# Relu² attention and a gated feed-forward layer on one core: the seventh batch's regrouping pieces stand 11 passes later in the fifth batch's part

## The chip, the cores and the metric

The kernel runs on one core of a Trainium2 chip. The metric is the time of one execution on the device in microseconds. The kernel before took 402.35 us, the median of three runs (401.11 to 404.22).

## The reference

There are 8 batches, 12 heads, 448 tokens and a head size of 64, so the feed-forward layer has 3584 tokens, a width of 768 and a hidden size of 1536. Inputs and output are float32.

```python
scores = scale * np.matmul(q, k.transpose(0, 1, 3, 2))
attn = np.maximum(scores, 0.0) ** 2 / S
attn_out = np.matmul(attn, v)
x = attn_out.transpose(0, 2, 1, 3).reshape(B * S, H * D)
gate = np.maximum(x @ w_gate, 0.0)
val = x @ w_val
out = gate * val @ w_out
```

## The kernel before

**The five engines.** TensorE (PE) multiplies matrices into PSUM banks; VectorE (DVE) and ScalarE (ACT) compute on and evict them; GpSimd (POOL) and SyncE (SP) mostly issue transfers. Each engine works through its own instructions in the order in which the kernel pins them (`pin`, line 68), and waits where an instruction's inputs are not there.

**Parts.** The loop over b, from 1 to 6, at lines 762 to 808, makes one part for each b. In part b PE computes the gate and value products of batch b-1 in 12 units (`gv_unit`, line 302), one for each 128 hidden columns. A unit is 12 passes, and a pass is four matmuls of 64 by 64 weights on 448 tokens (`mm4`, line 79). At its end ACT takes the relu of the gate (line 320) and DVE multiplies it with the value half into `hT` (line 321). Units take the PSUM bank pairs 6 and 4 in turn. Counted from zero, unit 9 and unit 11 therefore share a pair.

**Events.** Between the passes stand the attention's steps, each at a place (unit, pass). A score tile is one pass of matmuls from `kqT`, the transposed k and q, a relu by ACT (line 232) and a square by DVE (line 233). Seven of them make one group of four heads; a value event then runs seven passes of v on these squares, evicts them by ACT and DVE (lines 266 and 267) and exchanges halves with two DVE copies (line 261). `paced` spreads score and value events evenly over the part; `spread` sorts all events by place, keeping the order of those at the same place, and puts each ahead of that pass. In the part b = 4, called the fifth batch's part here, the fifth batch's scores and the first seven score tiles of the sixth are computed, and a last value event stands at (11, 5).

**Loads, regrouping and transposes.** From the third batch on, k and q come into `kn` and `qn` by POOL's transfers. Four regrouping pieces for a batch turn them: each is one DVE copy of half of k or q into `kr` or `qr` (`regroup`, line 180, 128 by 1536 elements), followed on SP's queue by two transposing transfers into `kqT` (`transpose_grouped`, line 188). `turned` places a batch's four pieces: two for k at a given place and five passes later, and two for q at another place and five passes later. `hold` (line 691) makes POOL read an element at the end of both halves of `kqT`, so that POOL issues the next batch's loads only when the transposes have landed. In the part b = 4, `hold(5)` and the load of the seventh batch's k and q (`load_qk(6)`) are placed at (5, 4), and the seventh batch's pieces behind them. The next part (b = 5) has `hold(6)` and the next load at (2, 1).

**The output products.** Behind part b = 4 stands `out_pair(2, ...)`, the output products of two batches in seven products for each 128 tokens instead of eight. Its products take PSUM banks 6, 7, 0, 1 and 2, 3, 4, 5. DVE makes the sums of `hT` for it (line 349): first S1 = A21 + A22, then S3 = A11 - A21 and S2 = S1 - A11. PE's first eight products need no sum; the next four use S2. ACT and DVE evict the results (lines 395 and 399), and POOL and SP store them (line 409).

Of the kernel before, what the change touches and what calls it, by code (L numbers as in the profile page):

```python
# [16 lines left out]
def kernel(  # L17
# [122 lines left out]
    def load_qk(b, h0=0, h1=H):  # L140
        load_nat(kn_b[natural(b)], k, b, h0, h1)
        load_nat(qn_b[natural(b)], q, b, h0, h1)

    def load_v(b):
        for c, p in HALVES:
            if b == 0:
                src = v[b].rearrange("(g c h) s d -> c h g s d", c=2, h=2)[c]
                dst = v_b[b % NB][p].rearrange("p (g h) i d -> p h g i d", h=2)
                parts = [(dst[:, h2], src[h2]) for h2 in range(2)]
            else:  # L150
                parts = [(v_b[b % NB][p], v[b, c * HP:c * HP + HP])]
            for dst, src in parts:
                dma_in(dst[:, :, 0:4, :], src[:, 0:256, :].rearrange("g (j i) d -> j g i d", i=4))
                dma_in(dst[:, :, 4:7, :], src[:, 256:448, :].rearrange("g (j i) d -> j g i d", i=3))
# [12 lines left out]
    def load_wo():  # L167
        for c in range(2):
            rows = moe_w_out[c * (d_ff // 2):(c + 1) * (d_ff // 2), :]
            dma_in(wo_sb[c], rows.rearrange("(kf p) m -> p kf m", p=128))  # L170
# [5 lines left out]
    def regroup(b, t, h):  # L176

        nat, grp = ((kn_b[natural(b)], kr), (qn_b[natural(b)], qr))[t]
        i = slice(2 * h, 2 * h + 2)
        pin(nc.vector.tensor_copy(grp.rearrange("p i (h d) -> p i h d", d=D)[:, i],  # L180
                                  nat.rearrange("p h i d -> p i h d")[:, i]))

    def transpose_grouped(b, t, h):

        grp = (kr, qr)[t]
        for i in (2 * h, 2 * h + 1):
            r = 128 if i < 3 else 64
            pin(nc.sync.dma_start_transpose(out=T_b[b % NB][:, t, :, i * 128:i * 128 + r], in_=grp[0:r, i, :]))
# [103 lines left out]
    def flat(t, n, c):  # L292

        names = " ".join("abcd"[:len(t.shape) - 1])
        return t.rearrange(f"p {names} -> p ({names})")[:, 0:n * c].rearrange("p (n c) -> p n c", c=c)

    def new_x(b):
        x = [xpool.tile([128, HP, S], BF16, name=f"x{n}") for n in range(2)]
        x_of[b] = [quads(t) for t in x]
        return x  # L300
# [40 lines left out]
    def weight_sums(n):  # L341

        o, a, b, op = ((T1, B12, B11, ALU.subtract), (B12, B22, B12, ALU.subtract),
                       (T2, B22, T1, ALU.subtract), (T4, B21, T2, ALU.subtract))[n]
        pin(nc.vector.tensor_tensor(o, a, b, op))
# [239 lines left out]
    def gv_units(b):  # L585
        b0 = b - b % 2
        if b == b0:
            hT_of[b0] = hpool.tile([128, KF, 2 * S], BF16, name="hT")
        return [gv_unit(b, mf, BEGUN, rotation((BEGUN_IN[mf],))) if b == 0 and mf < len(BEGUN_IN) else
                gv_unit(b, mf, BEGUN if mf == 0 else STRAIGHT, acc) for mf in range(KF)]  # L590
# [85 lines left out]
    def values_event(b, qd):  # L676
        return lambda: (values_by_parity if b >= B - 2 else values)(b, qd, sc_later())

    def transposes_event(b, qd):
        return lambda: transpose_quad(b, qd)  # L680
# [7 lines left out]
    def hold(b):  # L688

        for t in range(2):  # L690
            pin(nc.gpsimd.tensor_copy(flag[:, t:t + 1], T_b[b % NB][:, t, HP - 1, S - 1:S]))  # L691
# [26 lines left out]
    def step(units, u, n, k):  # L718
        at = len(units[-1]) * u + n + k
        return at // len(units[-1]), at % len(units[-1])  # L720

    def turned(b, units, *at):

        def piece(t, h):
            regroup(b, t, h)
            transpose_grouped(b, t, h)
        return [(*step(units, u, n, 5 * h), lambda t=t, h=h: piece(t, h)) for t, (u, n) in enumerate(at) for h in range(2)]

    def stream(b0, b1):

        e = []
        for b in range(b0, b1):
            for n in range(NT):
                if n % NC == 2 and (b, n) != (b0, 2):
                    vb, qd = (b, n // NC - 1) if n > NC else (b - 1, NQ - 1)
                    e.append((b, n, values_event(vb, qd), NC))
                e.append((b, n, scores_event(b, n), 1))
        return e

    def paced(units, first, behind, events):  # L740

        at = [(u, n) for u in range(len(units)) for n in range(len(units[u]))][first:behind]
        gaps = [{(1, 1): 1, (1, NC): 0.35, (NC, 1): 0.75}[a[3], b[3]] for a, b in zip(events, events[1:])]
        gap = len(at) / (sum(gaps) + 1)
        places, due = [], gap / 2
        for (*_, e, _), g in zip(events, gaps + [0]):
            u, n = at[int(due)]
            places.append((u, n, e))
            due += g * gap
        return places  # L750
# [5 lines left out]
    units = gv_units(0)  # L756
# [5 lines left out]
    for b in range(1, B - 1):  # L762
        if b < B - 3:
            new_x(b)
        units = units[2:] if b == 1 else gv_units(b - 1)
        last = len(units) - 1
        if b < B - 4:
            first, behind = {1: (24, 105), 2: (40, 132)}.get(b, (0, 132))
            events = paced(units, first, behind, stream(b, b + 1))
            events.append((last, 8 if b == 1 else 5, values_event(b, NQ - 1)))  # L770
        else:
            todo = [e for e in attention if e[:2] <= ENDS[b]]
            del attention[:len(todo)]
            if b == B - 4:
                begun = flat(kn_b[1], 4, S)
                x_of[b + 1] = [[begun[:, 2 * e:2 * e + 2, :]] for e in range(2)]
                del attention[[e[3] for e in attention].index(NC)]
            events = paced(units, 0, 144 if b == B - 3 else 132, todo)
            if b != B - 3:
                events.append((last, 5, values_event(*((b + 1, 0) if b == B - 4 else (B - 1, NQ - 1)))))  # L780
        if b == 1:
            events += [(1, 2 + 4 * qd, transposes_event(1, qd)) for qd in range(NQ)]
            events += turned(2, units, (last - 3, 7), (last - 2, 7))
            events += [(last, 2, lambda: (hold(2), load_v(2), load_wo(), load_qk(3)))]
        elif b == 2:
            events += [(1, 1, lambda: load_v(3))]
            events += [(last - 5 + 2 * n, 6, lambda n=n: weight_sums(2 * n)) for n in range(2)]
            events += [(last - 1 + t, 3 + 5 * h, lambda t=t, h=h: regroup(3, t, h)) for t in range(2) for h in range(2)]
            events += [(last, 10, lambda: [transpose_grouped(3, t, h) for t in range(2) for h in range(2)])]
        elif b == 3:  # L790
            events += [(2, 1, lambda: (hold_unit(2, 1), hold(3), load_qk(4), load_v(4)))]
            events += turned(4, units, (6, 1), (7, 1)) + [(8, 4, lambda: (hold(4), load_qk(5)))]
        elif b == 4:
            events += [(0, 4, lambda: load_v(5))]
            events += turned(5, units, (2, 1), (3, 1)) + [(5, 4, lambda: (hold(5), load_qk(6)))]
            events += turned(6, units, (last - 2, 6), (last - 1, 6))
        elif b == 5:
            events += [(2, 1, lambda: (hold_unit(4, 1), load_v(6), hold(6), load_qk(7)))]
            events += turned(7, units, (last - 4, 6), (last - 3, 6))
            later = [xpool.tile([128, HP, S], BF16, name=f"x{n}") for n in range(2)]  # L800
            x_of[b] = [x_of[b][e] + quads(later[e])[1:] for e in range(2)]
            x_of[B - 2] = [quads(t)[:1] for t in later]
        elif b == 6:
            events += [(3, 1, lambda: (hold(7), load_v(7)))]
            new = [xpool.tile([128, HP, S], BF16, name=f"x{n}") for n in range(2)]
            x_of[b] = [x_of[b][e] + quads(new[e])[1:] for e in range(2)]
            x_of[B - 1] = [quads(flat(t, HP, S)) for t in (kr, qr)]
        spread(units, events)
        if b == 2:
            out_pair(0, flat(kn_b[1], KH, S), [lambda: weight_sums(1), lambda: weight_sums(3)])  # L810
        elif b == 4:
            out_pair(2, flat(v_b[0], KH, S))
# [48 lines left out]
```

## Time and profile before

| | before |
|---|---|
| median of 3 runs | 402.35 us (401.11 to 404.22) |
| profiled execution, its own time | 403.33 us |
| its span, first to last instruction | 401.6 us |
| PE / DVE / ACT / POOL busy | 97% / 75% / 61% / 24% of the span |
| granted TensorE clock | 1.00 |
| DVE's regrouping copies, 24 of 128 by 1536 elements | 0.55 us each |

The profile shows one execution. Times in it are microseconds from the start of the span. PE, DVE, ACT, POOL and SP are the engines, and a q behind the name (SPq) means its queue of issued work. L180 is line 180 of the kernel. In a row of a timeline stand the start, the length, the engine and line, the operation, what it writes and reads, and how many instructions the row merges; in brackets stands the idle time of the engine just before it and what ended it. "issue" there means that the profile shows nothing that was waited for; a wait for a transfer's landing can hide behind it. A matmul's row ends when its last result is written; the next pass can start before that, so rows of PE overlap.

### The profile page before, as it was taken

To read this page: it belongs to the slowest core of one execution; us is meant where nothing else is said; L and a number is where in the kernel's file an instruction comes from. 1 tells how busy PE (TensorE), PEld (TensorE's weight loads), DVE (VectorE), ACT (ScalarE), POOL (GpSimd) and SP (SyncE) were. 2 spreads that over 40 slices of the span, in tenths; PEclk is the share of its full clock that TensorE was granted. 3 is DMA by queue.
4 is the path that set the end of the run, shared out by engine and by line. 5 is a ranking of instruction groups with operands and counts; after the bars stand their busy time and mean duration, and the time that the engine had idled before them with its cause. 6 is when DMAs were issued, how large, how long until landed. Compare 5 with 4: busy or idle time off the path is not lost.

```text
span 401.6 us, 16574 instructions
## 1 busy us (share of the span) xinstructions
PE 389.9 (97%) x7376; PEld 290.5 (72%) x7376; DVE 302.9 (75%) x530; ACT 243.6 (61%) x358; POOL 96.3 (24%) x168
## 2 busy tenths in 40 slices
PE   7899999999999999999899999999999999999995
PEld 3466779978776666679677666988887766777664
DVE  4985896699944696887781478988889969997922
ACT  3962994787334776988533588899883234344231
POOL 7933300810213600503031360020003230000223
PEclk9999999999999999999999999999999999999999
DMA  9999998999836894997963588770002350000036
GB/s 151 168 196 197 196 191 97 155 205 179 135 83 179 108 163 82 149 154 86 171 110 80 160 108 103 122 89 4 4 2 52 77 153 3 2 3 3 20 83 177
DMA packets 90872, 44.17 MB, mean 110 GB/s; under 512 B 55424, under 2 KB 89792, under 8 KB 90800
## 3 DMA queue, kind: packets, MB, share of 16 engines
q0 software_dynamic: 51264, 28.83, 50.5%
q1 hardware_dynamic: 39104, 13.99, 19.8%
q8 instruction: 57, 0.93, 1.0%
q10 hardware_dynamic: 432, 0.30, 0.3%
q14 instruction: 15, 0.12, 0.1%
HBM read 47.19 MB, written 11.01 MB: 145 GB/s over the span
## 4 chain that ended last, share of the span: by engine, by line
PE 86%; DMA 5%; DVE 5%; issue 1%; ACT 1%; POOL 1%; ACTq 0%; DVEq 0%; POOLq 0%
PE ps L72 85%; DMA qn<-in_q_dram 5%; DVE attn L233 2%; ACT r_sb L232 1%; PE ps L208 1%; DVE kqT L209 1%; POOL kn L116 1%; POOL qn L116 0%; DVE x L267 0%; DVE hT L321 0%; DVE r_sb L630 0%; DVE x L653 0%; PE ps L217 0%; DVE x L261 0%; ACT g_sb L320 0%
## 5 line engine op out<-in xcount | busy, mean ns | idle before, releaser
L72 PE MATMUL ps<-x,gv 64*64 64x448 bf16 x3408 | 198.4, 349 | 1.2 <-DVE hT L321 0.9
L72 PEld LDWEIGHTS <-gv 64*64 64x64 bf16 x4032 | 150.5, 107 | 44.5 <-issue 2.9
L232 ACT ACTIVATE r_sb<-ps 128x896 bf16<-128x896 f32 x167 | 149.0, 933 | 17.7 <-PE ps L72 15.0
L233 DVE TENSOR_TENSOR attn<-r_sb 128x896 bf16<-128x896 bf16 x167 | 101.9, 622 | 29.2 <-ACT r_sb L232 22.0
L409 POOL DMA_DIRECT2D out_dram<-attn x63 | 33.1, 530 | 170.0 <-DVE attn L399 134.6
L72 PE MATMUL ps<-kqT 64*64 64x448 bf16 x672 | 68.6, 351 | 3.4 <-ACT r_sb L232 2.6
L72 PEld LDWEIGHTS <-hT 128*64 128x64 bf16 x1056 | 55.9, 110 | 20.9 <-issue 1.4
L395 ACT ACTIVATE attn<-ps 128x384 f32<-128x384 f32 (+1 forms) x64 | 28.8, 450 | 64.3 <-PE ps L72 63.3
L72 PE MATMUL ps<-wo,hT 128*64 128x384 bf16 (+1 forms) x720 | 54.3, 306 | 0.0
L321 DVE TENSOR_TENSOR hT<-ps,g_sb 128x448 bf16<-128x448 f32 x72 | 44.5, 619 | 8.3 <-ACT g_sb L320 7.5
L320 ACT ACTIVATE g_sb<-ps 128x448 bf16<-128x448 f32 x72 | 39.2, 546 | 17.3 <-PE ps L72 17.1
L399 DVE TENSOR_TENSOR attn<-ps,attn 128x384 f32<-128x384 f32 (+1 forms) x48 | 22.8, 503 | 33.0 <-ACT attn L395 18.4
L72 PEld LDWEIGHTS <-vn 64*64 64x64 bf16 (+1 forms) x888 | 35.8, 107 | 12.3 <-issue 2.3
L72 PEld LDWEIGHTS <-kqT 64*64 64x64 bf16 x672 | 28.3, 106 | 14.1 <-issue 6.0
L72 PE MATMUL ps<-attn,vn 64*64 64x448 bf16 x672 | 37.8, 350 | 0.7 <-DVE attn L233 0.7
L528 ACT ACTIVATE kqT<-ps 128x896 f32<-128x896 f32 x18 | 16.5, 918 | 25.0 <-PE ps L72 25.0
L116 POOL DMA_DIRECT2D vn<-in_v_dram x36 | 23.7, 678 | 17.8 <-PE ps L72 5.8
L72 PE MATMUL ps<-o_ring,hT 128*64 128x384 bf16 (+1 forms) x336 | 26.0, 306 | 0.0
L532 DVE TENSOR_TENSOR kqT<-ps,kqT 128x896 f32<-128x896 f32 x18 | 19.5, 1086 | 5.9 <-PE ps L72 4.2
L691 POOL COPY flag<-kqT 128x1 bf16<-128x1 bf16 x12 | 2.2, 197 | 89.7 <-DMA kqT<-kr 48.3
L116 POOL DMA_DIRECT2D qn<-in_q_dram x20 | 14.8, 762 | 1.3 <-POOLq L845 0.8
L261 DVE COPY x<-x 64x896 bf16<-64x896 bf16 x34 | 13.5, 397 | 1.8
(101 smaller groups left out, 288.5 us busy)
## 6 DMA issues: line engine op xcount, KB each, us to landing
out_dram<-attn POOLq DMA_DIRECT2D x48, 96.0 KB, 2.3
out_dram<-attn SPq DMA_DIRECT2D x48, 96.0 KB, 2.6
kn<-in_k_dram POOLq DMA_DIRECT2D x7, 384.0 KB, 6.8
qn<-in_q_dram POOLq DMA_DIRECT2D x7, 384.0 KB, 9.2
vn<-in_v_dram POOLq DMA_DIRECT2D x14, 192.0 KB, 8.8
gv<-in_moe_w_gate_dram POOLq DMA_DIRECT2D x6, 384.0 KB, 11.6
gv<-in_moe_w_val_dram POOLq DMA_DIRECT2D x6, 384.0 KB, 11.8
wo<-in_moe_w_out_dram POOLq DMA_DIRECT2D x2, 1152.0 KB, 13.7
```

The source lines that it names most:

```text
L72: pin(nc.tensor.matmul(o, lhsT=l, rhs=r, start=start, stop=stop, skip_group_check=True))
L116: pin(nc.gpsimd.dma_start(out=o, in_=i))
L232: pin(nc.scalar.activation(r, src, AF.Relu))
L233: pin(nc.vector.tensor_tensor(dst, r, r, ALU.mult))
L261: pin(nc.vector.tensor_copy(x1[p], x0[other]))
L320: pin(nc.scalar.activation(g_sb, o[0], AF.Relu, scale=float(out_scale)))
L321: pin(nc.vector.tensor_tensor(hT[:, mf, col:col + S], o[1], g_sb, ALU.mult))
L395: pin(nc.scalar.activation(out_of(t, r, c), bank(P, t), AF.Copy))
L399: pin(nc.vector.tensor_tensor(o, bank(Q, t), o, ALU.add))
L409: pin(engines[c].dma_start(out=rows[:, c0:c1, :], in_=src))
L528: pin(nc.scalar.activation(held(n, j), both(PQ[n][0]), AF.Copy))
L532: pin(nc.vector.tensor_tensor(k, both(PQ[n][1]), k, ALU.add))
```

## The change

One line differs, in the part b = 4. `last` is 11, the number of the last unit.

```diff
             events += turned(5, units, (2, 1), (3, 1)) + [(5, 4, lambda: (hold(5), load_qk(6)))]
-            events += turned(6, units, (last - 2, 6), (last - 1, 6))
+            events += turned(6, units, (last - 1, 5), (last, 5))
```

The pieces for k move from the places (9, 6) and (9, 11) to (10, 5) and (10, 10); those for q move from (10, 6) and (10, 11) to (11, 5) and (11, 10). Each place is 11 passes later. The first q piece shares its place with the last value event, and stands behind it. The instructions and their count are the same, and on PE, ACT, POOL and SP so is their order; on DVE the four copies stand later in the order. The place of the load, (5, 4), is not changed, nor is the place of `hold(6)` in the next part.

## The prediction

> **What bounds the kernel now.** I read the page's busy times first, then the chain that ended last, and then that chain in order of time.
>
> ```profile
> span 401.6 us, 16574 instructions
> ...
> PE 389.9 (97%) x7376; PEld 290.5 (72%) x7376; DVE 302.9 (75%) x530; ACT 243.6 (61%) x358; POOL 96.3 (24%) x168
> ...
> PE 86%; DMA 5%; DVE 5%; issue 1%; ACT 1%; POOL 1%; ACTq 0%; DVEq 0%; POOLq 0%
> ```
>
> PE is busy for 97% of the span and is 86% of the chain, so a change pays only what it takes out of, or adds to, PE's idle places. A DMA share of 5% on a chain that PE otherwise owns is odd. The chain in order of time shows where part of it lies:
>
> ```profile
> 188.01 0.73 POOL qn L116
> 188.75 6.70 DMA qn<-in_q_dram
> ...
> 197.05 0.81 issue
> 197.85 0.10 DVE qr L180
> ...
> 198.33 0.63 DVE attn L233
> ...
> 199.00 31.18 PE ps L72 x477
> ```
>
> The load of the seventh batch's q, issued at 188.01 and 188.75, passes to the regrouping copy qr of line 180 at 197.85, on to a square of line 233, and on to PE at 199.00. So the moved pieces stand on the path. PE there, from the timeline (start, length, what, how many; in brackets the idle time before and who ended it):
>
> ```profile
> 191.00 1.27 PE L72 MATMUL ps<-x,gv 64*64 64x448 bf16 x20
> ...
> 194.22 0.95 PE L72 MATMUL ps<-x,gv 64*64 64x448 bf16 x14
> 196.03 1.13 PE L72 MATMUL ps<-x,gv 64*64 64x448 bf16 x18 [0.87 <-DVE hT L321]
> 196.82 1.48 PE L72 MATMUL ps<-attn,vn 64*64 64x448 bf16 x24
> 199.00 0.38 PE L72 MATMUL ps<-attn,vn 64*64 64x448 bf16 x4 [0.70 <-DVE attn L233]
> 199.19 1.52 PE L72 MATMUL ps<-x,gv 64*64 64x448 bf16 x28
> 200.64 7.03 PE L72 MATMUL ps<-wo,hT 128*64 128x384 bf16 x96
> ```
>
> A pass is four matmuls. From 191.00 to 194.22 lie 17 passes (68 matmuls, three score tiles among them), 0.189 us each. From 194.22 to 200.64 lie 14+18+24+4+28 = 88 matmuls, 22 passes, which at 0.189 are 4.17 us; they took 6.42. Of the 2.25 us lost, 0.12 is the handover to the output products (seven passes from 199.19 end at 200.52). **The two waits cost 2.13 us** (1.09 from 194.22 to 196.82, where 8 passes took 2.60; 1.04 from 196.82 to 199.19, where 7 took 2.37), more than their 0.87 and 0.70, since an idle time is counted from the drained end of the last matmul. DVE in the same stretch says why:
>
> ```profile
> 191.02 0.62 DVE L321 TENSOR_TENSOR hT<-ps,g_sb 128x448 bf16<-128x448 f32 x1
> 191.56 0.62 DVE L233 TENSOR_TENSOR attn<-r_sb 128x896 bf16<-128x896 bf16 x1
> 193.88 0.56 DVE L180 COPY kr<-kn 128x1536 bf16<-128x1536 bf16 x1 [1.71 <-issue]
> 194.36 0.62 DVE L233 TENSOR_TENSOR attn<-r_sb 128x896 bf16<-128x896 bf16 x1
> ...
> 195.36 0.62 DVE L321 TENSOR_TENSOR hT<-ps,g_sb 128x448 bf16<-128x448 f32 x1
> ...
> 197.85 0.56 DVE L180 COPY qr<-qn 128x1536 bf16<-128x1536 bf16 x1 [0.81 <-issue]
> 198.33 0.62 DVE L233 TENSOR_TENSOR attn<-r_sb 128x896 bf16<-128x896 bf16 x1
> ...
> 199.33 0.62 DVE L321 TENSOR_TENSOR hT<-ps,g_sb 128x448 bf16<-128x448 f32 x1
> ...
> 200.58 0.79 DVE L261 COPY kn<-kn 64x896 bf16<-64x896 bf16 x2
> 201.40 0.62 DVE L321 TENSOR_TENSOR hT<-ps,g_sb 128x448 bf16<-128x448 f32 x1
> ...
> 205.02 1.62 DVE L349 TENSOR_TENSOR hT<-vn,hT 128x1344 bf16<-128x1344 bf16 x2
> ```
>
> The kr copy stands 1.71 us, the qr copy 0.81 us, each until its load has landed (k by 193.88, q by 197.85). Behind kr, in DVE's order, is the gate product of the tenth of twelve units (line 321 at 195.36), whose PSUM bank the last gate unit needs: PE's first wait ends at 196.03, as that instruction ends. Behind qr is the last square (198.33), which the seventh value pass needs: PE's second wait.
>
> **The change part by part.** It removes and adds no instruction; PE, ACT, POOL and SP keep their order. Four DVE copies move by 11 passes, and the eight transposes on SP's queue follow them in time. DVE's new order from 191.56 is: three squares with the line 321 between the first and the second of them behind 191.56, kr, square, kr, line 321, the value eviction (267, 261 twice), qr, qr, line 321, the sums of line 349. What feeds it, from ACT:
>
> ```profile
> 190.41 1.91 ACT L232 ACTIVATE r_sb<-ps 128x896 bf16<-128x896 f32 x2
> 192.22 0.54 ACT L320 ACTIVATE g_sb<-ps 128x448 bf16<-128x448 f32 x1
> 192.64 2.85 ACT L232 ACTIVATE r_sb<-ps 128x896 bf16<-128x896 f32 x3
> 195.39 0.54 ACT L320 ACTIVATE g_sb<-ps 128x448 bf16<-128x448 f32 x1
> 199.41 0.54 ACT L266 ACTIVATE kn<-ps 128x448 bf16<-128x448 f32 x1 [3.49 <-PE ps L72]
> ```
>
> ACT is back to back here and does not wait for DVE, so its times stand. Step by step:
> - First wait. The square behind 191.56 can go at 192.32 (190.41 + 1.91), line 321 at 192.9 (its input ends at 192.76), done by 193.5. The last gate unit wants that bank at 194.79 (194.22 and three passes). Cover 1.3 us: the wait goes, 1.09 of the 2.13.
> - kr at its new place. The squares go at 193.6 and 194.6 (ACT's three end near 193.6, 194.6, 195.49), kr at 195.1, square 195.6, kr 196.1, line 321 at 196.6 to 197.2. k landed at 193.88: cover 1.2 us, cost nothing.
> - Second wait. PE opens the last unit at 194.79, the values after five passes at 195.74, the seventh value pass at 196.88. The last square ends at 196.2, 0.7 us earlier: the wait goes, 1.04 of the 2.13.
> - qr. PE ends the values near 197.07 and the unit at 198.39; the products open at 198.5 instead of 200.64. The eviction runs 197.3 to 198.8 (199.41 less 199.00 behind the last value pass, then 0.69 and 0.79), qr at 198.75 and 199.25, line 321 at 199.75, the sums from 200.3. q landed by 197.85: cover 0.9 us.
> - What is late next. The sums began at 201.94 (201.40 and one spacing of 0.54), 1.30 behind PE's handover; now 1.8 behind it, 0.5 later against PE. Who waits for them is the product with S2, which PE opens here:
>
> ```profile
> 207.50 0.82 PE L72 MATMUL ps<-o_ring,hT 128*64 128x384 bf16 x8
> ```
>
> S2's first half was ready at 205.87 for 207.50 and its second at 206.64 for 207.93 (three of the product's six row blocks on); the smaller cover of 1.29 becomes 0.8. Cost nothing; without cover, each further microsecond costs one.
> - SP and POOL. Their queues (SP first):
>
> ```profile
> 194.51 5.39 SPq L188 DMA_TRANSPOSE kqT<-kr  x4
> 199.99 6.14 SPq L188 DMA_TRANSPOSE kqT<-qr  x4
> 216.63 10.69 SPq L409 DMA_DIRECT2D out_dram<-attn  x16
> ```
>
> ```profile
> 207.40 4.22 POOL L409 DMA_DIRECT2D out_dram<-attn  x8 [17.86 <-DVE attn L399]
> ...
> 235.38 0.36 POOL L691 COPY flag<-kqT 128x1 bf16<-128x1 bf16 x2
> ```
>
> The eight transposes took from 194.51 to 206.13; from kr at 195.1 and qr at 198.8 on, and at the same rates, they end near 207. SP's next work, the stores of 216.63, comes near 214.5: nothing is queued behind them in time. POOL's marks at 235.38, which hold the next loads back until the transposes have landed, come near 233.3, some 26 us behind the last transposes: nothing. POOL stands idle for 17.86 us, from the q loads' issue until the stores near 205, so the moved copies pass none of its issues.
>
> Bounds from rows. The gain can't pass the 2.25 us lost in the stretch; if both waits return in full it is nothing, and with a late q below nothing. I take 2.1, near the upper end, as all four covers are 0.7 us or more. All PE work behind 200.64 follows from PE's own order (the chain gives PE 31.18 us unbroken from 199.00), so the gain is kept. The profiled execution took 403.33 us for its span of 401.6, 1.0 above the median of 402.35 (401.11 to 404.22). By the sum the span becomes 399.5, that execution 401.2, and the median **400.2 us**.
>
> **One rule weighed.** The trace shows kr's transposes on SP (from 194.51) running while the q load was still out (to 197.85). By rows alone q may land where it did, and the cover at qr is 0.9 us. The Trainium skill, DMA: Bandwidth & Descriptors, "Issuing engines are not separate DMA queues", says that transfers issued by different engines run on the same DMA engines and interleave. By that, q would land a little earlier, as the transposes start about 1.2 us later, and the sum stays at 2.1 with a safer cover; against the change, the qr transposes would share with the first output stores near 205, which is rival C.
>
> **The rivals.**
> - A, the forecast: both waits go, 400.2. For it: four covers of 0.7 to 1.3 us.
> - B, one wait stays: q lands late enough for DVE to stand at qr, or the square of 195.6 comes too late for the value pass (cover 0.7). About 1.09 us is gained: 401.3. Against it: q's landing is an issue at fixed place and only 0.9 us of cover are asked of it.
> - C, the gain is given back at the next part's first square, which already stood 1.73 us for a store:
>
> ```profile
> 226.90 1.37 DVE L233 TENSOR_TENSOR attn<-r_sb 128x896 bf16<-128x896 bf16 x2 [1.73 <-DMA out_dram<-attn]
> ```
>
> The transposes now reach the stores' time, the stores land late, and PE is held up there by what was gained. It decides once that wait grows by 2 us. Against it: the last transposes end 18 us ahead, and the stores it waits for are the last ones. 402.3.
> - D, slower: the sums of line 349 come too late for the S2 product, since qr now stands before them. PE then waits at 207.50's place. It decides once q lands after 198.75 + 0.8 + 2.1 = 201.7, 3.9 us later than in this trace; at 203.2 the time is 403.9. For it: the q loads' landings elsewhere in this trace are widely spread:
>
> ```profile
> DMA to landing us min/median/max: 4.6/8.8/20.1
> ```
>
> Against it: the same load, at the same place, landed within 9.1 us of its second issue (188.75 to 197.85), a median one. The change itself can't fail to be made: the order of the instructions shows it.
>
> **How the numbers follow.** A 0.76, B 0.12, C 0.07, D 0.05. A's own range is 1.5 to 2.25 us of gain, with about 0.8 for the spread of a median of few runs that differ by 3 us: 399.2 to 401.6. To 401.9 it takes in most of B; below, 399.0. C, most of D and the tails are left out, 2 in 10. One per cent, about what a measurement of this kernel can tell from no change, is 4.0 us, beyond 398.3 and 406.4. No case gives 4 us of gain by its mechanism, so faster is 0.04 (spread of the runs alone); slower needs D with q 8 us late, 0.02; same 0.94.
>
> **What would show it.** Right: no idle time ahead of kr and qr, line 321 of the tenth unit ending near 193.5, PE unbroken from 191.00 to the products, which open near 198.5, S2's product 6.9 us after them. B would show an idle time ahead of qr, or PE waiting for line 233 at the values; C a longer wait of line 233 for a store in the next part, with PE behind it; D PE waiting for line 349. The prediction is wrong if PE's waits of this stretch turn up elsewhere on its row, or if the loads' landing differs by microseconds between executions.

## The result and the profile after

The changed kernel takes 400.81 us, the median of 22 runs (399.43 to 402.46); the kernel before, run beside it, 402.66 us (401.11 to 404.75, 22 runs). The medians differ by 1.85 us. The ratio of the means is 0.9949, with a 95% interval of 0.9934 to 0.9964: 2.1 us faster, between 1.4 and 2.7. The forecast was 400.2 and 2.1 us. The profiled execution took 400.31 us for a span of 398.5.

The page of the changed kernel has these lines against those of before:

```profile
span 398.5 us, 16574 instructions
...
PE 389.0 (98%) x7376; PEld 278.4 (70%) x7376; DVE 303.4 (76%) x530; ACT 243.6 (61%) x358; POOL 96.9 (24%) x168
...
PE 93%; DVE 3%; DMA 1%; POOL 1%; issue 0%; ACT 0%; POOLq 0%; ACTq 0%
```

PE's share of the chain rose from 86% to 93%, and the DMA share fell from 5% to 1%: the link through the q load is gone. In the chain of this execution, in order of time, one piece now covers the whole stretch:

```profile
183.87 46.31 PE ps L72 x801
```

PE's timeline in the stretch:

```profile
190.13 1.11 PE L72 MATMUL ps<-x,gv 64*64 64x448 bf16 x20
...
193.34 1.68 PE L72 MATMUL ps<-x,gv 64*64 64x448 bf16 x32
194.86 1.49 PE L72 MATMUL ps<-attn,vn 64*64 64x448 bf16 x28
196.18 1.49 PE L72 MATMUL ps<-x,gv 64*64 64x448 bf16 x28
197.61 7.03 PE L72 MATMUL ps<-wo,hT 128*64 128x384 bf16 x96
204.47 3.59 PE L72 MATMUL ps<-o_ring,hT 128*64 128x384 bf16 x48
```

The rows that were cut in two by waits (14 and 18 matmuls, 24 and 4) are whole: 32 and 28. From the row of 20 to the output products PE took 9.64 us before (191.00 to 200.64) and takes 7.48 now (190.13 to 197.61). **The stretch gives 2.16 us.** The spans differ by 3.1, which is more than the change did: 0.87 us of it lie ahead of the stretch, where the two programs are the same: executions differ there by themselves (in the profiles of the two kernels and of experiments 1 to 4, whose programs are the same up to there, the row of 20 starts between 189.64 and 191.84). Behind the stretch the difference grows by 0.07 (401.6 and 398.5, less 3.03 at the products).

DVE's timeline in the stretch of the changed kernel:

```profile
191.89 0.62 DVE L321 TENSOR_TENSOR hT<-ps,g_sb 128x448 bf16<-128x448 f32 x1
...
194.17 0.55 DVE L180 COPY kr<-kn 128x1536 bf16<-128x1536 bf16 x1
194.64 0.62 DVE L233 TENSOR_TENSOR attn<-r_sb 128x896 bf16<-128x896 bf16 x1
195.18 0.55 DVE L180 COPY kr<-kn 128x1536 bf16<-128x1536 bf16 x1
...
197.98 1.03 DVE L180 COPY qr<-qn 128x1536 bf16<-128x1536 bf16 x2
198.92 0.62 DVE L321 TENSOR_TENSOR hT<-ps,g_sb 128x448 bf16<-128x448 f32 x1
199.46 1.62 DVE L349 TENSOR_TENSOR vn<-hT 128x1344 bf16<-128x1344 bf16 x2
...
202.53 1.62 DVE L349 TENSOR_TENSOR hT<-vn,hT 128x1344 bf16<-128x1344 bf16 x2
...
224.36 1.16 DVE L233 TENSOR_TENSOR attn<-r_sb 128x896 bf16<-128x896 bf16 x2 [2.22 <-DMA out_dram<-attn]
```

No copy of line 180 has an idle time in brackets. The gate product that PE's last unit waited for now ends at 192.5, not at the moment when PE needs it.

### The profile page after: what moved, and what is told of

The parts are those of the page before. It is cut to its first block, busy times and chain, and to the rows that moved or that the text cites. A ratio compares the mean times of both kernels' runs of the same rounds, so it can differ in the third digit from the quotient of the medians.

```text
span 398.5 us, 16574 instructions
## 1 busy us (share of the span) xinstructions
PE 389.0 (98%) x7376; PEld 278.4 (70%) x7376; DVE 303.4 (76%) x530; ACT 243.6 (61%) x358; POOL 96.9 (24%) x168
## 4 chain that ended last, share of the span: by engine, by line
PE 93%; DVE 3%; DMA 1%; POOL 1%; issue 0%; ACT 0%; POOLq 0%; ACTq 0%
PE ps L72 92%; DVE attn L233 2%; DMA qn<-in_q_dram 1%; PE ps L208 1%; DVE kqT L209 1%; POOL qn L116 0%; ACT r_sb L232 0%; POOL kn L116 0%; DVE x L653 0%; DVE attn L399 0%; POOL ident L112 0%; POOLq L112 0%; ACTq L232 0%; POOLq L845 0%
## 5 line engine op out<-in xcount | busy, mean ns | idle before, releaser
L72 PEld LDWEIGHTS <-gv 64*64 64x64 bf16 x4032 | 140.2, 107 | 53.2 <-issue 2.2
L72 PE MATMUL ps<-kqT 64*64 64x448 bf16 x672 | 66.1, 351 | 3.0 <-ACT r_sb L232 2.6
L72 PEld LDWEIGHTS <-vn 64*64 64x64 bf16 (+1 forms) x888 | 34.4, 107 | 12.5 <-issue 1.2
L72 PEld LDWEIGHTS <-kqT 64*64 64x64 bf16 x672 | 25.9, 106 | 14.8 <-issue 5.3
```

The lines of the kernel that those rows point to most:

```text
L72: pin(nc.tensor.matmul(o, lhsT=l, rhs=r, start=start, stop=stop, skip_group_check=True))
```

## The experiments

Two explanations fit a gain of this size. The theory of the prediction is that DVE stood for the landing of the loads, with PE's next inputs queued behind it. The rival is that four copies of half a microsecond, 2.0 us in all, stood in a stretch where DVE has no room, so that moving them away pays by itself. Unless another count is given, times are medians; each kernel was timed beside the kernel before on the same chip. The ratio in brackets, with its 95% interval, is not quite the quotient of the two medians.

**1. Old places, nothing to wait for.** The kernel before, with one edit; the seventh batch's scores come from wrong data:

```diff
-        nat, grp = ((kn_b[natural(b)], kr), (qn_b[natural(b)], qr))[t]
+        nat, grp = ((qn_b[1] if b == 6 else kn_b[natural(b)], kr),
+                    (qn_b[1] if b == 6 else qn_b[natural(b)], qr))[t]
```

> The kernel before, its pieces at their old places, but the seventh batch's regrouping copies read a buffer that has long been resident (the weight sums in the second q buffer) instead of the k and q just loaded, so nothing waits for the load's landing; the load itself is still made. The seventh batch's scores are then made from wrong k and q. Theory (the wait for the loads is what is paid): PE's two waits before the output products go, 2.1 us faster than before, about the time of the changed kernel (400.8 against 402.7). Rival (four copies of half a microsecond stood in a stretch where DVE has no room, and moving them out is what pays): no gain, 402.7.

400.13 us against 402.57 (ratio 0.9950, 0.9927 to 0.9973). Its DVE timeline has the copies where they were, without the waits:

```profile
190.62 0.55 DVE L180 COPY kr<-qn 128x1536 bf16<-128x1536 bf16 x1
191.09 0.62 DVE L233 TENSOR_TENSOR attn<-r_sb 128x896 bf16<-128x896 bf16 x1
191.62 0.56 DVE L180 COPY kr<-qn 128x1536 bf16<-128x1536 bf16 x1
192.09 0.62 DVE L321 TENSOR_TENSOR hT<-ps,g_sb 128x448 bf16<-128x448 f32 x1
```

and PE takes the same 7.48 us for the stretch as in the changed kernel:

```profile
189.64 1.12 PE L72 MATMUL ps<-x,gv 64*64 64x448 bf16 x20
...
197.12 5.07 PE L72 MATMUL ps<-wo,hT 128*64 128x384 bf16 x66
```

Four copies in the full stretch cost PE nothing. The rival falls; the whole gain is the wait for data.

**2. The k pieces alone, and 3. the q pieces alone.** The kernel before with one line each:

```diff
-            events += turned(6, units, (last - 2, 6), (last - 1, 6))
+            events += turned(6, units, (last - 1, 5), (last - 1, 6))   # 2: k alone
+            events += turned(6, units, (last - 2, 6), (last, 5))       # 3: q alone
```

> Only the k pieces move (to (10, 5) and (10, 10)); the q pieces stay at (10, 6) and (10, 11). Theory: the first wait of PE goes, but the last square still stands behind the first q copy and so behind the q load's landing near 197.8, a time that PE does not set; the second wait grows from 1.04 to about 2.1 us and nothing is gained: within 0.3 us of before. Rival (copies out of a full stretch): two of four copies leave the ninth and tenth units, about 1 us faster. If each wait were worth its own share, as a plain sum of the two has it: 1.09 us faster.

402.57 against 402.57 (ratio 1.0000, 0.9974 to 1.0026). DVE, then PE, of this kernel:

```profile
196.02 0.55 DVE L180 COPY kr<-kn 128x1536 bf16<-128x1536 bf16 x1
199.45 0.56 DVE L180 COPY qr<-qn 128x1536 bf16<-128x1536 bf16 x1 [2.88 <-issue]
199.93 0.62 DVE L233 TENSOR_TENSOR attn<-r_sb 128x896 bf16<-128x896 bf16 x1
```

```profile
195.06 1.83 PE L72 MATMUL ps<-x,gv 64*64 64x448 bf16 x32
196.57 1.46 PE L72 MATMUL ps<-attn,vn 64*64 64x448 bf16 x24
200.60 0.38 PE L72 MATMUL ps<-attn,vn 64*64 64x448 bf16 x4 [2.58 <-DVE attn L233]
```

The first wait is gone (a row of 32), and the second has grown from 0.70 to 2.58 us: PE came sooner to a square that comes no sooner, since q's landing does not depend on PE. This execution, at 404.95 us, is the slowest of its twelve, and part of the growth is its own: qr starts 7.61 us behind the start of the row of 20 (191.84) instead of 6.85, and the stretch up to the output products takes 10.40 us (to 202.24) instead of 9.64. It is longer by just the 0.76 us by which q is later: the stretch follows q's landing, and not k's place.

> Only the q pieces move (to (11, 5) and (11, 10)); the k pieces stay at (9, 6) and (9, 11). Theory: the first wait of PE stays (DVE stands for k until about 193.9, PE until 196.0) and the second goes: 1.0 us faster than before. Rival (copies out of a full stretch): also about 1 us, but then the second kernel of this call must show the same.

401.91 against 402.57 (ratio 0.9972, 0.9945 to 1.0000), 0.7 us faster by the medians for the 1.0 expected, and just short of certain. PE of this kernel:

```profile
194.86 1.13 PE L72 MATMUL ps<-x,gv 64*64 64x448 bf16 x18 [1.04 <-DVE hT L321]
195.65 1.67 PE L72 MATMUL ps<-attn,vn 64*64 64x448 bf16 x28
```

The first wait stays and the second is gone. The stretch takes 8.92 us (189.66 to 198.58), 0.72 less than before. The two single moves give 0 and 0.7 us, both together 1.85. The intervals of the single moves are 1 us wide on either side, so the times alone would not settle it; with the rows they do: the waits are one behind the other on loads with their own time, and are not two prices to be added.

**4. How much the new place still hides.** The changed kernel with each q copy made three times:

```diff
-            regroup(b, t, h)
+            [regroup(b, t, h) for _ in range(3 if (b, t) == (6, 1) else 1)]
```

> The changed kernel with each of the two q copies made three times in a row, so four more copies of about 0.5 us, 2.0 us in all, ahead of the last gate product and the sums of line 349. It tests what the place behind the value eviction still covers. By the changed kernel's trace the second half of S2 has 0.75 us of cover: PE then waits 1.2 to 1.3 us ahead of the S2 product, and the gain over before falls from 1.85 to about 0.6 us. If the sums had no bearing on PE: as fast as the changed kernel. If there were no cover at all: all of the 2.0 us is lost, and the kernel is no faster than before.

402.65 against 402.57 (ratio 1.0006, 0.9985 to 1.0028). DVE, then PE, of this kernel:

```profile
198.75 3.41 DVE L180 COPY qr<-qn 128x1536 bf16<-128x1536 bf16 x6
202.08 0.62 DVE L321 TENSOR_TENSOR hT<-ps,g_sb 128x448 bf16<-128x448 f32 x1
...
205.68 1.62 DVE L349 TENSOR_TENSOR hT<-vn,hT 128x1344 bf16<-128x1344 bf16 x2
```

```profile
198.42 7.03 PE L72 MATMUL ps<-wo,hT 128*64 128x384 bf16 x96
206.59 3.89 PE L72 MATMUL ps<-o_ring,hT 128*64 128x384 bf16 x48 [1.14 <-DVE hT L349]
```

Six copies take 3.33 us to the next instruction, two took 0.94 (197.98 to 198.92): the four more cost 2.39, not 2.0. PE opens the S2 product 8.17 us behind the first products instead of 6.86, 1.31 later, and takes 0.30 longer in it, as its second half waits too: 1.61 lost, and 2.39 less 1.61 is a cover of 0.78, against 0.75 in the trace. So the cover is real and thin, and the forecast for the run (0.6 us of gain left) missed by the copies' length: 1.85 less 1.61 leaves 0.24, which this run can't tell from none.

**5. The load later.** The changed kernel, with POOL's load held by the ninth unit's product:

```diff
-... + [(5, 4, lambda: (hold(5), load_qk(6)))]
+... + [(9, 1, lambda: (hold_unit(3, 8), hold(5), load_qk(6)))]
```

> The changed kernel with its pieces at the new places, but POOL issues the seventh batch's k and q load only when the gate product of the ninth unit (index 8) of this part is done: about 190.8 in the changed kernel's profile instead of 185.76, 5.0 us later. Theory (what DVE waits for is the load's landing): k lands near 197.9 and q near 202.1; DVE stands again at kr (3.7 us) and PE waits about 3.0 us for the last square, then about 0.5 us at the sums: 3.5 us slower than the changed kernel, 404.3. Rival (copies out of a full stretch are what paid): as fast as the changed kernel, 400.8.

405.34 against 402.64 (ratio 1.0057, 1.0031 to 1.0083), 4.5 us above the changed kernel's 400.81. POOL issued the load at 191.46; DVE, then PE, then PE's clock in three windows (after the length: busy time of PE, PEld, DVE, ACT and POOL, then the granted clock, the DMA share and GB/s):

```profile
198.15 0.56 DVE L180 COPY kr<-kn 128x1536 bf16<-128x1536 bf16 x1 [3.82 <-DMA kn<-in_k_dram]
```

```profile
199.29 0.38 PE L72 MATMUL ps<-attn,vn 64*64 64x448 bf16 x4 [3.04 <-DVE attn L233]
199.48 2.67 PE L72 MATMUL ps<-x,gv 64*64 64x448 bf16 x28
202.08 7.51 PE L72 MATMUL ps<-wo,hT 128*64 128x384 bf16 x96
209.43 0.82 PE L72 MATMUL ps<-o_ring,hT 128*64 128x384 bf16 x8
```

```profile
190.00:195.00 5.00, 5.00 (x114) 5.00 (x108) 3.62 (x7) 4.79 (x7) 3.68 (x7) 1.00 0.42 48
199.00:202.10 3.10, 2.81 (x34) 1.50 (x33) 2.85 (x7) 0.54 (x1) 0.00 (x0) 0.61 1.45 211
202.10:206.00 3.90, 3.90 (x51) 2.74 (x50) 3.90 (x7) 1.80 (x4) 0.00 (x0) 0.87 0.99 146
```

Here the profile names the releaser of kr outright, the k load. The waits at kr and at the last square are as forecast, 3.8 us on DVE and 3.04 on PE; the half microsecond at the sums did not come, as the S2 product at 209.43 has no wait. What made the run slower than forecast is a slower TensorE: from the row behind the wait to the output products PE took 2.60 us (199.48 to 202.08) instead of 1.43 in the changed kernel, at a granted clock of 0.61 over that window, and from there to the S2 product 7.35 instead of 6.86. These are 1.17 and 0.49 us, beside 3.35 for the wait itself (199.29 less 195.94, where the seventh value pass was due): 5.0 in this profile, 4.5 in the medians.

**6. One more set of pieces later.** The changed kernel with the third batch's q pieces 4 passes later:

```diff
-            events += turned(2, units, (last - 3, 7), (last - 2, 7))
+            events += turned(2, units, (last - 3, 7), (last - 2, 11))
```

> The changed kernel with one more set of pieces moved: the third batch's two q pieces stand 4 passes later in the second batch's part. In the profiles here DVE stands 0.3 to 1.2 us for the q load at the first of them, and PE 0.5 to 0.9 us behind it in two of six profiles. Theory: what is left of those waits goes, 0.2 to 0.5 us faster than the changed kernel (400.3 to 400.6), hardly more than these runs can tell. If the pieces are not what PE waits for there: no change, 400.8.

400.34 against 402.64 (ratio 0.9929, 0.9903 to 0.9956). The interval holds the changed kernel's ratio (0.9949), so no further gain is shown. The wait that it was to remove is not in every execution: the first of the two copies stood 0.34 us for the q load in the changed kernel's profile, 0.87 in experiment 2's and 1.21 in experiment 4's; in those of the kernel before and experiments 1 and 3 no wait is listed, and none here. The median of this kernel is the lowest of the kernels that leave nothing out.

**7. The load sooner.** The kernel before without the hold:

```diff
-... + [(5, 4, lambda: (hold(5), load_qk(6)))]
+... + [(5, 4, lambda: load_qk(6))]
```

> The kernel before, pieces at the old places, without the two reads with which POOL holds the seventh batch's load back until the sixth batch's transposes have landed; the load is then issued some 11 us sooner, near 174.6 instead of 186.5. Theory: the waits at kr and qr go (2.1 us), but the load now runs beside the q transposes of the sixth batch, which landed only 0.3 us ahead of the score tile that needs them (185.9 for 186.27); if they are slowed by x us PE waits about x us there. I expect x between 1 and 4: 401.5 to 404.5, and no idle time of DVE ahead of the seventh batch's pieces. If DMA sharing cost the transposes nothing: 400.5, as the changed kernel.

409.93 against 402.64 (ratio 1.0156, 1.0112 to 1.0201), worse than all of the range expected. The seventh batch's pieces stand for nothing any more, but the sixth batch's transposes are late. POOL issued the load even sooner than the 174.6 expected, k at 168.73 and q at 173.46, each as soon as a regrouping copy of the sixth batch had read the buffer, so that it ran beside the sixth batch's k transposes too. The landing times of the sixth batch's eight transposes in the kernel before and in this one, then PE and its clock in this one:

```profile
DMA to landing us min/median/max: 3.9/5.1/8.8
```

```profile
DMA to landing us min/median/max: 3.6/10.7/14.2
```

```profile
191.91 0.59 PE L72 MATMUL ps<-kqT 64*64 64x448 bf16 x4 [6.06 <-DMA kqT<-qr]
```

```profile
191.90:197.40 5.50, 5.49 (x60) 3.18 (x64) 1.25 (x2) 1.83 (x2) 0.00 (x0) 0.50 0.01 3
```

PE lost 6.4 us at the score tile (five passes from 184.56 end at 185.5) and 2.7 more at half clock (15 passes in 5.53 us instead of 2.84). Less the 2.1 us of the waits at the pieces, that is 7.0; measured are 7.3 by the medians (6.3 by the ratio, four runs). The loads were slowed as well: they landed in 12.2 to 15.9 us, against 5.1 to 9.0 in the kernel before. The hold protects the transposes, and the price of it is a late load; moving the pieces pays that price where DVE has time.

## Why the prediction was right

- **The sum.** The 2.13 us forecast for the two waits came out as 2.16 in the profiles, and 1.85 in the medians (1.4 to 2.7). Right, by its mechanism, as experiments 1 and 5 show from both sides. That 2.16 is so near to 2.13 says less than it seems, as both use the same execution of the kernel before; that the price holds for other executions is what the interval says. The time of 400.2 was 0.6 too low: 0.3 is the kernel before, whose median over 22 runs is 402.66 and not 402.35, and the rest the gain.
- **First wait.** The gate product was to be done by 193.5 for a need at 194.79, a cover of 1.3. It ends at 192.5 for 193.91 (193.34 and three passes): 1.4.
- **Second wait.** The cover of 0.7 for the last square: it ends at 195.3 for the value pass at 196.0, 0.7.
- **qr.** The copies start as soon as the eviction ends, and q (issued at 188.0, landed in 9.1 us) was there 0.9 us before, as forecast.
- **The loads' landing.** A difference of microseconds between executions was to count against the prediction. In the two kernels' profiles and those of experiments 1 to 4, q landed 8.6 to 9.6 us behind its second issue. The latest is 0.5 us behind the changed kernel's 9.1 and would still leave 0.4 of the cover at qr. In the kernel before, where DVE stands for it, such a delay goes straight into PE's wait (experiment 2).
- **What is late next.** The sums begin 1.85 behind PE's handover (199.46 less 197.61), for 1.8 forecast; the cover of the S2 product is 0.75, for 0.8. Experiment 4 used it up.
- **SP and POOL.** The transposes and what follows, from SP and POOL of the changed kernel:

```profile
194.79 6.54 SPq L188 DMA_TRANSPOSE kqT<-kr  x4
201.42 5.46 SPq L188 DMA_TRANSPOSE kqT<-qr  x4
213.60 11.23 SPq L409 DMA_DIRECT2D out_dram<-attn  x16
```

```profile
232.36 0.35 POOL L691 COPY flag<-kqT 128x1 bf16<-128x1 bf16 x2
```

They end at 206.9, 6.7 us ahead of SP's next store, and POOL's marks don't wait. The k transposes took 6.54 us in place of 5.39, so "at the same rates" was not quite so; there was room for it.
- **The rule weighed.** q was to land a little sooner with fewer transposes beside it. Its landings were 7.8 to 9.0 us before and 7.7 to 9.1 after: no such effect is seen, and it was not needed. The rule itself (the Trainium skill, DMA: Bandwidth & Descriptors, "Issuing engines are not separate DMA queues") agrees with experiment 7, where the loads beside the transposes doubled their median landing from 5.1 to 10.7 us.
- **Rival C** did not come: the square behind the stores stands 2.22 us instead of 1.73, and PE doesn't wait behind it. **Rival D**'s wait at the sums came only where experiment 4 forced it.
- **What was loose.** The prediction gave 1.09 and 1.04 us as the shares of two waits, and rival B took a single wait to be worth its share. Experiment 2 shows that it is not: with the q wait left in place the k wait is worth nothing. The chain of before pointed there, as of the two loads it names only q's. It was not proof: its row of the q load ends at 195.45, where line 321 follows, and only time listed as issue leads to qr at 197.85. That q had landed just then comes from its own landing, 9.0 us behind 188.75.

## What to carry to other kernels

An engine that works in order and stands for a load makes all that is queued behind it late; move the waiting instruction behind what the bounding engine needs next, to a place where the data have landed and its successors still have cover, and count the landing and the cover in the same timeline. Two waits one behind the other are not summed: the one that hangs on the later outside event decides, so follow the chain and undo that one first. Sooner loads are no free remedy where they share the engines with transfers that are themselves just in time.

## What the runs showed of the hardware

TensorE's clock fell after a long wait. After the waits of 0.87 and 0.70 us in the kernel before, the granted clock from 196.0 to 200.6 was 1.00, and after one of 2.58 us it was 1.00 from 200.6 to 204.0 (experiment 2); after one of 3.04 us it was 0.61 over 3.1 us and 0.87 over the next 3.9 (experiment 5), and after one of 6.06 us it was 0.50 over 5.5 us (experiment 7). That added 1.7 us and 2.7 us to waits that had cost 3.4 and 6.4. The row of the kernel before:

```profile
196.00:200.60 4.60, 3.87 (x74) 2.44 (x73) 3.69 (x8) 0.54 (x1) 0.00 (x0) 1.00 0.98 150
```

The Trainium skill, TensorE: Matmul & The Clock Gate, Part 1, says that the array falls to half rate after an idle window of about 3.4 us and returns to full rate after a busy one. The half rate agrees with experiment 7; in experiment 5 it came after an idle row of 3.04 us, a little less than the window, counted from the drained end of the last matmul (3.35 us from the place of the next pass).
